# Key-product masks split between ScalarE and GpSimd, and the inverse's share per step changed

## The chip, the cores and the metric

The kernel runs on one core of a Trainium2 chip. The metric is device time in microseconds (us) from launch to end: the median of three runs of the kernel before is 1092.77 us (1090.2 to 1094.73). Engines: TensorE (PE; PEld its weight loads), VectorE (DVE), ScalarE (ACT), GpSimd (POOL) and SyncE (SP), which issues most DMAs.

## The reference

Three stages in float32: a linear recurrence per head (4 x 8 heads, 768 steps, head dimension 40), a mixture of experts, and a squared-ReLU feed-forward layer. Only the first is touched:

```python
for t in range(S):
    y[:, :, t] = einsum('bhd,bhde->bhe', rt, state)
    Sa = einsum('bhde,bhe->bhd', state, at)
    state_decay = state * wt[:, :, None, :] - einsum('bhd,bhe->bhde', Sa, bt)
    state = state_decay + einsum('bhd,bhe->bhde', vt, kt)
```

## The kernel before

The recurrence is cut into 24 chunks of 32 time steps, and four chunks make a slab. Within a chunk the recurrence is solved in closed form: the products of `k` and `b` with `a` give two 32 x 32 blocks a head, of which only the strictly lower triangles count (key products: rows 64 to 95 for `k`, rows 96 to 127 for `b`, the latter with the sign changed). The `b` block is inverted as a triangular matrix, one slab (four chunks of 32 heads, 128 partitions) at a time.

Names. `L(c)` makes the key products of chunk c: `heads` issues 32 matmuls of 40x64x32 (64 in the trace, fp32 counts twice) into the one PSUM tile `pr`, and then masks them into `zs` of that chunk; a DMA stores the `b` block in DRAM (`nt`), a later one (`tul`) reads it back turned into `tu`, on which `inv` works. `RUV` uses the same `heads` and the same `pr` for the products with `r` (R products), masked into `ym`; `Y` also writes to `pr`. So R, Y and the key products take turns in `pr`, and each must be evacuated before the next begins. `post` copies `a` into rows 0 to 39 of `zs` on ScalarE. `prod` scales `a` and `kb` of a chunk by decay products made by `decay` (four scans on VectorE for two chunks). In a chunk's own step `Zst`, `UTst`, `Ust`, `KBt`, `Sst`, `Stt` and `Y` do the matmul work, with ScalarE evacuating most of it and VectorE the state (`m`).

Every engine works in the order in which the program lists its instructions. That order is written out by hand: `ORD` lists, for a slab's first, second, third and fourth step (chunk index modulo 4), the stages of TensorE; behind each stage `pump` releases a number of places of a schedule, into which side work is put: `PA` says at which step, place and on which engines (V or G) `prod` of each chunk of the slab after next is issued, `LP` behind which stage its `L` stands. The first two `L` of a slab stand in the fourth step two slabs earlier, the other two in the first step of the slab before. `IB` gives the part of the inverse (in a planner's cost units) taken into each step: none in the first, the rest in the fourth. `IB0` does the same for the first slab's steps. The inverse for the next slab runs in a slab's second, third and fourth step.

In the profile below the steps are numbered by chunk: step 10 is a slab's third, step 11 its fourth, step 12 the first of the next slab.

Of the kernel before, what the change touches and what calls it, by code (L numbers as in the profile page):

```python
# [12 lines left out]
ALU = mybir.AluOpType  # L13
AF = mybir.ActivationFunctionType
# [3 lines left out]


class Attn:  # L20
    IB=(0, 6, 5, 99)
    IB0=(0, 7.5, 5.5, 99)
    I0=1
    PT=(2, 14)
# [2 lines left out]
    F2=5  # L27
    F3=0
    CA=(1, 2, 20)
    PA=((2, 11, 'VGG'), (2, 12, 'GGG'), (4, 4, 'VGG'), (4, 11, 'VGG'))  # L30
    CB=(3, 0, 20)
    SC=(2, 14)
    L0=('R', 'K0')
# [6 lines left out]
    def __init__(s, tc, ins, NC, ctx, ident, pctx=None, side=None):  # L40
        s.tc=tc; s.nc=nc=tc.nc; s.ins=ins; s.NC=NC; s.NS=NC//4
        P=lambda name,**k: ctx.enter_context(tc.tile_pool(name=name,**k))
        cp=s.cp=P('attn_c',bufs=1); cq=(pctx or ctx).enter_context(tc.tile_pool(name='attn_p',bufs=1,side=side))
        s.ps=P('aps',bufs=6,space=PSUM); s.psy=P('psy',bufs=1,space=PSUM)
        s.dram=P('adr',bufs=3,space=DRAM)
        T=lambda n,sh: cp.tile(sh,F32,tag=n,name=n)
        Tq=lambda n,sh: cq.tile(sh,F32,tag=n,name=n)
        def ring(n,k,sh,early=0): return [(Tq if i<early else T)(f'{n}{i}',sh) for i in range(k)]

        s.W=ring('w',2,[104,2,32,18],2); s.A=ring('a',4,[104,16,32],4); s.KB=ring('kb',8,[104,16,64],4)  # L50
        s.Pp=ring('pp',6,[104,2,32,18],4); s.Q=ring('qq',2,[104,2,32,18],2)
        s.one=Tq('one',[104,32,18]); s.inv_=Tq('inv',[104,32,18])
        s.ZS=ring('zs',8,[128,32,32],4)
        s.YS=T('ys',[128,32,40]); s.VU=T('vu',[128,32,40]); s.M1=T('m1',[128,32,64])
        s.YM=T('ym',[128,32,32]); s.R=T('r',[104,16,32]); s.UT=T('ut',[128,16,64]); s.UTc=T('utc',[128,2,256])
        s.TT=T('tt',[128,8,128]); s.TU=Tq('tu',[128,1024]); s.tmp=Tq('tmp',[128,256])
        s.Z=T('z',[128,8,64]); s.XT=T('xt',[104,4,16,32]); s.DL=ring('dl',12,[40,32])
        s.PR=s.psy.tile([128,2,512],F32,tag='pr',name='pr'); s.PY=[s.PR[:,i,256:512] for i in range(2)]
        s.ident=ident
        s.fill=[]; s.nt={}; s.td={}  # L60

        s.load_w(0); s.load_w(1); s.load_a(0); s.load_k(0); s.load_a(1); s.load_k(1)
        for c in (2,3): s.load_a(c); s.load_k(c)
        V=nc.vector; G=nc.gpsimd
        G.memset(s.one,0.0); G.memset(s.one[:,:,0:1],1.0); G.memset(s.one[:,:,17:18],1.0); G.memset(s.inv_,0.0)
        G.memset(s.TT,0.0)
        make_identity(nc,ident)
        s.mask=T('mask',[128,2,32])
        G.memset(s.mask,1.0); G.memset(s.mask[96:128,0],-1.0)
        for b in (64,96):  # L70
            G.affine_select(out=s.mask[b:b+32],in_=s.mask[b:b+32],pattern=[[0,2],[1,32]],compare_op=ALU.is_ge,fill=0.0,base=-1,channel_multiplier=-1)
        for t in s.ZS[0:2]: s.zero(t[32:64])
# [20 lines left out]
    r=0  # L93
# [36 lines left out]
    def post(s,c):  # L130
# [4 lines left out]
        if c:  # L135
            d=s.g(s.DL,c).rearrange('p (x r) -> p x r',r=2); pp=s.pslice(c-1)
            V.tensor_tensor(out=d[:,:,0],in0=pp[0:40,:,1,16],in1=q[0:40,:,0,0],op=ALU.mult)
            V.tensor_tensor(out=d[:,:,1],in0=pp[64:104,:,1,16],in1=q[64:104,:,0,0],op=ALU.mult)
    def heads(s,w,x,out,mask):

        nc=s.nc; pt=s.PR
        for p in range(8):
            for hf in range(2):
                for r in range(2):
                    k=slice(64*r,64*r+40)
                    nc.tensor.matmul(pt[64*hf:64*hf+64,r,32*p:32*p+32],w[k,8*hf+p,:],x[k,8*hf+p,:],start=True,stop=True)  # L146
        for hf in range(2):
            nc.vector.tensor_tensor(out=out[64:128,16*hf:16*hf+16].rearrange('p (x r) t -> p x r t',r=2),  # L148
                in0=pt[64*hf:64*hf+64,:,0:256].rearrange('p r (x t) -> p x r t',t=32),
                in1=mask.unsqueeze(1).unsqueeze(1).to_broadcast([64,8,2,32]),op=ALU.mult)  # L150
    def L(s,c,store=True):
        nc=s.nc; a=s.g(s.A,c); kb=s.g(s.KB,c); zs=s.g(s.ZS,c)
        s.heads(kb,a,zs,s.mask[64:128,0])
        sl=c//4
        if c%4==0: s.nt[sl]=s.dram.tile([4,32,32,32],F32,tag='nt',name='nt')
        if store: nc.sync.dma_start(s.nt[sl][c%4],zs[96:128])
        s.post(c); s.load_a(c+4)
# [105 lines left out]
    def run(s, sink, more=None, before=None):  # L263
# [27 lines left out]
        for c in range(NC):  # L291
# [18 lines left out]
            for P in (sl+1,sl+2):  # L310
# [4 lines left out]
                for k in range(4):  # L315
                    e,p,w=s.PA[k]
                    if d==e: at(p,lambda x=2*A+k,w=w: s.prod(x,eng(w)))
# [3 lines left out]
            if nx:  # L321
                ib=s.IB if sl else s.IB0
                if r==s.I0 if sl else r==1: s.invq=s.inv(sl+1)
# [530 lines left out]
```

## Time and profile before

| | us |
|---|---|
| median of three runs | 1092.77 |
| profiled execution | 1089.77 |
| its span | 1088.0 |
| PE, DVE, ACT, POOL busy | 911.3, 691.4, 463.8, 319.8 |

The span is the time from the first to the last instruction of one execution; the profiled execution's own time is 1.8 us longer. The chain of work that ended last is by 63% on PE, 16% on DVE, 5% on ACT and 2% on POOL. The recurrence takes the first 555 us or so; one slab of it repeats in steps 10 to 13, from 277.5 to 362.9. Busy time is an average over stages with different limits, so the steps are read one by one.

### The profile page before, as it was taken

How to read it: one execution, taken by the hardware profiler on the slowest of the kernel's cores; microseconds unless marked ns; L12 is line 12 of the kernel's file. 1: busy time of each engine (PE TensorE's matmuls, PEld its weight loads, DVE VectorE, ACT ScalarE, POOL GpSimd, SP SyncE). 2: the span in 40 equal slices, each digit the busy share in tenths (PEclk: the TensorE clock that was granted, in tenths of full speed). 3: DMA queues.
4: the chain of work that ended last, by engine and by line, in shares of the span. 5: the costliest groups of instructions: out<-in, count | busy, mean ns of one | idle time of the engine just before them, and what ended most of it. 6: DMA issues, size and time to landing. Idle time of an engine off the chain costs nothing.

```text
span 1088.0 us, 30273 instructions
## 1 busy us (share of the span) xinstructions
PE 911.3 (84%) x12696; PEld 867.5 (80%) x12696; DVE 691.4 (64%) x1621; ACT 463.8 (43%) x1016; POOL 319.8 (29%) x292
## 2 busy tenths in 40 slices
PE   1238978878978976998948989869999999999996
PEld 1227877777867866887848989869999999999996
DVE  7997967966875875864659988746444434443331
ACT  6324543543443443545536546424333333333331
POOL 6031512511521425536554223352121111100000
PEclk9999866866876876687859999989999999999999
DMA  7548674474464444459549887820011111000000
GB/s 183 129 105 237 185 186 119 114 189 114 117 165 113 110 115 126 107 152 261 146 141 256 285 300 254 251 83 20 25 30 31 30 31 31 28 29 13 13 12 17
DMA packets 128134, 132.05 MB, mean 121 GB/s; under 512 B 80201, under 2 KB 104559, under 8 KB 127987
## 3 DMA queue, kind: packets, MB, share of 16 engines
q1 hardware_dynamic: 123731, 118.95, 39.6%
q0 software_dynamic: 4256, 11.06, 3.1%
q8 instruction: 102, 1.67, 0.6%
q14 instruction: 45, 0.37, 0.1%
HBM read 104.79 MB, written 29.70 MB: 124 GB/s over the span
## 4 chain that ended last, share of the span: by engine, by line
PE 63%; DVE 16%; issue 6%; DMA 6%; ACT 5%; POOL 2%; SPq 1%; another core or an unknown queue 0%; ACTq 0%; DVEq 0%; POOLq 0%
PE fps L554 19%; PE fps L561 17%; PE ps L241 7%; PE pr L146 4%; PE ps L219 3%; PE pr L259 3%; PE ps L405 3%; PE ps L250 2%; PE ps L210 2%; DMA c<-in_w_out 2%; DVE tu L175 2%; DVE tmp L174 2%; POOL kb L129 1%; DVE ym L148 1%; DMA kb<-in_kb 1%
## 5 line engine op out<-in xcount | busy, mean ns | idle before, releaser
L554 PE MATMUL fps<-xl,w1h 128*128 128x256 f32 x768 | 198.8, 286 | 8.7 <-DVE xl L544 8.6
L554 PE MATMUL fps<-xh,w1h 128*128 128x256 f32 x768 | 199.8, 287 | 4.8 <-ACT xh L543 4.2
L561 PE MATMUL fps<-w2h,hh 128*128 128x320 f32 x512 | 158.7, 310 | 0.0
L561 PE MATMUL fps<-w2h,hl 128*128 128x320 f32 x512 | 158.2, 309 | 0.0
L561 PE MATMUL fps<-w2l,hh 128*128 128x320 f32 x512 | 158.1, 309 | 0.0
L554 PEld LDWEIGHTS fps<-xl,w1h 128*128 128x128 f32 x768 | 148.9, 194 | 10.5 <-DVE xl L544 10.5
L554 PEld LDWEIGHTS fps<-xh,w1h 128*128 128x128 f32 x768 | 148.7, 194 | 6.3 <-ACT xh L543 5.3
L662 DVE TENSOR_TENSOR g<-r 128x512 f32<-128x512 f32 x96 | 68.8, 716 | 81.0 <-ACT r L661 81.0
L664 DVE TENSOR_TENSOR hl<-g,hh 128x512 fp32r<-128x512 f32 x96 | 74.8, 779 | 66.0 <-ACT hh L663 65.3
L146 PE MATMUL pr<-a,kb 40*64 40x32 f32 x1536 | 43.2, 280 | 74.8 <-issue 29.8
L554 PE MATMUL fps<-xh,w1l 128*128 128x256 f32 x512 | 103.7, 284 | 0.0
L146 PEld LDWEIGHTS pr<-a,kb 40*64 40x64 f32 x1536 | 40.6, 206 | 78.4 <-issue 48.8
L663 ACT CAST hh<-g 128x512 fp32r<-128x512 f32 x96 | 59.6, 621 | 94.1 <-DVE g L662 94.1
L241 PEld LDWEIGHTS ps<-vu,ys 128*40 128x40 f32 x1472 | 89.0, 163 | 13.2 <-ACT ys L213 6.2
L241 PE MATMUL ps<-vu,ys 128*40 128x40 f32 x1472 | 94.3, 249 | 5.3 <-ACT ys L213 3.4
L561 PEld LDWEIGHTS fps<-w2l,hh 128*128 128x128 f32 x512 | 96.1, 188 | 0.0
L561 PEld LDWEIGHTS fps<-w2h,hh 128*128 128x128 f32 x512 | 96.1, 188 | 0.0
L561 PEld LDWEIGHTS fps<-w2h,hl 128*128 128x128 f32 x512 | 96.1, 188 | 0.0
L661 ACT ACTIVATE r<-fps 128x512 f32<-128x512 f32 x96 | 57.1, 595 | 76.6 <-PE fps L554 76.6
L554 PEld LDWEIGHTS fps<-xh,w1l 128*128 128x128 f32 x512 | 80.5, 194 | 0.0
L175 DVE TENSOR_TENSOR tu<-tu,tmp 128x120 f32<-128x120 f32 (+25 forms) x312 | 80.3, 292 | 0.0
L174 DVE TENSOR_TENSOR tmp<-tu 128x120 f32<-128x120 f32 (+25 forms) x312 | 74.5, 272 | 0.5
(143 smaller groups left out, 1739.8 us busy)
## 6 DMA issues: line engine op xcount, KB each, us to landing
kb<-in_kb SPq DMA_DIRECT2D x24, 416.0 KB
ut<-in_vE SPq DMA_DIRECT2D x24, 416.0 KB
raw<-in_w SPq DMA_DIRECT2D x16, 512.0 KB
raw<-in_w SPq DMA_DIRECT2D x16, 480.0 KB
w<-in_w SPq DMA_DIRECT2D x12, 468.0 KB
a<-in_a SPq DMA_DIRECT2D x24, 208.0 KB
r<-in_r SPq DMA_DIRECT2D x24, 208.0 KB
c<-in_w_out SPq DMA_DIRECT2D x7, 640.0 KB
```

The lines of the kernel that those rows point to most:

```text
L146: nc.tensor.matmul(pt[64*hf:64*hf+64,r,32*p:32*p+32],w[k,8*hf+p,:],x[k,8*hf+p,:],start=True,stop=True)
L174: if k==0: V.tensor_tensor(out=tv,in0=Tv[:,j:j+1,b0:b0+n].to_broadcast([128,j,n]),in1=Tv[:,0:j,j:j+1].to_broadcast([128,j,n]),op=ALU.mult)
L175: else: V.tensor_tensor(out=w,in0=w,in1=tv,op=ALU.add)
L219: nc.tensor.matmul(pt[32*i:32*i+32,40*j:40*j+40],zs[:,h,:],m[:,h,0:40],start=True,stop=True)
L241: nc.tensor.matmul(pt[k][0:40,40*n:40*n+40],ys[:,h,:],m[:,h,:],start=True,stop=True)
L259: nc.tensor.matmul(pt[64*par:64*par+40,32*(k//2):32*(k//2)+32],ys[:,h,:],ym[:,h,:],start=True,stop=True)
L554: nc.tensor.matmul(pt[:,256*u:256*u+256],a,b,start=i==0,stop=i==len(ops)-1)
L561: nc.tensor.matmul(pt[:,0:320],a,b,start=first and n==0,stop=last and n==23); n+=1
L661: nc.scalar.activation(out=r,in_=v,func=AF.Relu)
L662: V.tensor_tensor(out=g,in0=r,in1=r,op=ALU.mult)
L663: nc.scalar.copy(out=gh[:,2*m2:2*m2+2],in_=g)
L664: V.tensor_tensor(out=gl[:,2*m2:2*m2+2],in0=g,in1=gh[:,2*m2:2*m2+2],op=ALU.subtract)
```

## The change

Three edits. `heads` gets an argument `later`, true for the key products of chunks 4 to 23: instead of two VectorE multiplications by a mask of 0, 1 and -1, two ScalarE instructions copy the products from PSUM with a scale for each partition (`sgn`, 1 or -1), and two GpSimd instructions then set the part on and above the diagonal to zero in SBUF, 32 partitions each, the `b` block first. `IB` takes 8 instead of 5 units of the inverse in a slab's third step. `PA` gives the product of `a` of each slab's fourth chunk (from chunk 11 on) to GpSimd.

```diff
-    IB=(0, 6, 5, 99)
+    IB=(0, 6, 8, 99)
-    PA=((2, 11, 'VGG'), (2, 12, 'GGG'), (4, 4, 'VGG'), (4, 11, 'VGG'))
+    PA=((2, 11, 'VGG'), (2, 12, 'GGG'), (4, 4, 'VGG'), (4, 11, 'GGG'))
...
+        s.sgn=T('sgn',[128,1]); G.memset(s.sgn,1.0); G.memset(s.sgn[96:128],-1.0)
...
-    def heads(s,w,x,out,mask):
+    def heads(s,w,x,out,mask,later=False):
...
+        if later:
+            for hf in range(2):
+                nc.scalar.activation(out=out[64:128,16*hf:16*hf+16].rearrange('p (x r) t -> p x r t',r=2),
+                    in_=pt[64*hf:64*hf+64,:,0:256].rearrange('p r (x t) -> p x r t',t=32),func=AF.Copy,scale=s.sgn[64:128])
+            for b in (96,64):
+                nc.gpsimd.affine_select(out=out[b:b+32],in_=out[b:b+32],pattern=[[0,32],[1,32]],compare_op=ALU.is_ge,fill=0.0,base=-1,channel_multiplier=-1)
+            return
...
-        s.heads(kb,a,zs,s.mask[64:128,0])
+        s.heads(kb,a,zs,s.mask[64:128,0],c>3)
```

VectorE in the third step (step 10), around the mask of the R products (`ym`); `tu` and `tmp` are the inverse's, `a_87` the product of `a` for chunk 16, `m` the state's evacuation. Before:

```order
L174 TENSOR_TENSOR tmp<-tu 128x128
L174 TENSOR_TENSOR tmp<-tu 128x112
L175 TENSOR_TENSOR tu<-tu,tmp 128x16x8
L175 TENSOR_TENSOR tu<-tu,tmp 128x16x7
L148 TENSOR_TENSOR ym<-pr,mask 64x512 x2
L174 TENSOR_TENSOR tmp<-tu 128x119 x2
L175 TENSOR_TENSOR tu<-tu,tmp 128x17x7 x2
L408 TENSOR_REDUCE sm_198<-ps 128x9
L174 TENSOR_TENSOR tmp<-tu 128x126
L244 TENSOR_TENSOR m_119<-ps,dl_140 40x2x4x40 x2
```

And the same place of the changed kernel, whose lines stand some eight further down in the file:

```order
L182 TENSOR_TENSOR tmp<-tu 128x114 x2
L183 TENSOR_TENSOR tu<-tu,tmp 128x19x6 x2
L156 TENSOR_TENSOR ym<-pr,mask 64x512 x2
L182 TENSOR_TENSOR tmp<-tu 128x120
L182 TENSOR_TENSOR tmp<-tu 128x100
L183 TENSOR_TENSOR tu<-tu,tmp 128x20x6
L183 TENSOR_TENSOR tu<-tu,tmp 128x20x5
L182 TENSOR_TENSOR tmp<-tu 128x105
L416 TENSOR_REDUCE sm_201<-ps 128x9
L182 TENSOR_TENSOR tmp<-tu 128x105
L183 TENSOR_TENSOR tu<-tu,tmp 128x21x5
L252 TENSOR_TENSOR m_119<-ps,dl_140 40x2x4x40 x2
```

The inverse's columns 17 to 19 (four instructions each) moved from behind the R mask to ahead of it, and seven of its instructions stand between the mask and the first `m` where there were five.

GpSimd from the fourth step (step 11) into the first of the next slab (step 12); `xt` is the output's scaling, `kb` and `a` the products of later chunks, `xr`, `gt` and `xs` belong to the routing. Before:

```order
L262 TENSOR_TENSOR xt<-xt,pp_104 104x256 x2
L409 COPY xr_197<-xr_197 128x64
L129 TENSOR_TENSOR kb_93<-kb_93,qq_106 104x16x32 x2
L409 COPY xr_197<-xr_197 128x64
L129 TENSOR_TENSOR kb_94<-kb_94,qq_106 104x16x32 x2
L450 COPY gt_201<-xr_197 128x4
L428 DMA xs<-xr_197,slot 2048x388 x4
```

And after the change:

```order
L270 TENSOR_TENSOR xt<-xt,pp_104 104x256 x2
L153 AFFINE_SELECT zs_109<-zs_109 32x1024 x2
L153 AFFINE_SELECT zs_110<-zs_110 32x1024 x2
L417 COPY xr_200<-xr_200 128x64
L130 TENSOR_TENSOR kb_93<-kb_93,qq_106 104x16x32 x2
L417 COPY xr_200<-xr_200 128x64
L127 TENSOR_TENSOR a_90<-a_90,pp_102 104x512
L130 TENSOR_TENSOR kb_94<-kb_94,qq_106 104x16x32 x2
L153 AFFINE_SELECT zs_111<-zs_111 32x1024 x2
L153 AFFINE_SELECT zs_112<-zs_112 32x1024 x2
L458 COPY gt_204<-xr_200 128x4
L436 DMA xs<-xr_200,slot 2048x388 x4
```

Eight selects and one product of `a` came in, two selects behind each chunk's key products.

ScalarE in the first step (step 12), from the evacuation of U (`vu`) to the transposes of keys and state (`ys`), which the state products read. Before:

```order
L235 COPY vu<-ps 32x4x40 x8
L133 COPY zs_111<-a_89 40x16x32
L134 COPY zs_111<-a_89 40x16x32
L133 COPY zs_112<-a_90 40x16x32
L134 COPY zs_112<-a_90 40x16x32
L213 COPY ys<-ps 64x4x80 x2
L252 COPY ys<-ps 40x8x40 x2
```

And after the change:

```order
L243 COPY vu<-ps 32x4x40 x8
L150 ACTIVATE zs_111<-pr,sgn 64x512 x2
L134 COPY zs_111<-a_89 40x16x32
L135 COPY zs_111<-a_89 40x16x32
L150 ACTIVATE zs_112<-pr,sgn 64x512 x2
L134 COPY zs_112<-a_90 40x16x32
L135 COPY zs_112<-a_90 40x16x32
L221 COPY ys<-ps 64x4x80 x2
L260 COPY ys<-ps 40x8x40 x2
```

The copies of `a` moved behind the evacuation of each chunk's key products, and the transposes behind both.

## Rows read from the trace of the kernel before

**Rows 1.** Windows of steps 10, 11, 12: length, busy us (count) by engine, granted clock.

```profile
277.50:291.45 13.95, 12.66 (x314) 11.45 (x313) 10.88 (x34) 8.48 (x25) 9.78 (x8) 0.96 0.56 137
291.45:317.87 26.42, 19.62 (x475) 17.91 (x473) 21.49 (x68) 11.06 (x29) 8.38 (x5) 0.74 0.49 132
317.87:340.62 22.75, 18.58 (x416) 17.18 (x413) 13.09 (x37) 10.55 (x28) 2.75 (x4) 0.70 0.66 159
```

**Rows 2.** Timeline, TensorE, steps 11 and 12: start, length, work [idle before, releaser].

```profile
296.55 1.14 PE L146 MATMUL pr<-a,kb 40*64 40x32 f32 x64
302.54 1.90 PE L146 MATMUL pr<-r,ut 40*64 40x32 f32 x64 [2.84 <-DVE zs L148]
308.03 1.94 PE L146 MATMUL pr<-a,kb 40*64 40x32 f32 x64 [2.71 <-DVE ym L148]
327.57 1.94 PE L146 MATMUL pr<-a,kb 40*64 40x32 f32 x64 [2.00 <-DVE ym L148]
336.42 4.27 PE L241 MATMUL ps<-vu,ys 128*40 128x40 f32 x64
```

**Rows 3.** Timeline, VectorE, steps 10 to 12.

```profile
282.24 0.46 DVE L175 TENSOR_TENSOR tu<-tu,tmp 128x128 f32<-128x128 f32 x2
285.60 1.39 DVE L148 TENSOR_TENSOR ym<-pr,mask 64x512 f32<-64x512 f32 x2 [2.89 <-ACT vu L235]
287.02 1.69 DVE L174 TENSOR_TENSOR tmp<-tu 128x119 f32<-128x119 f32 x2
288.64 1.50 DVE L175 TENSOR_TENSOR tu<-tu,tmp 128x119 f32<-128x119 f32 x2
...
306.49 1.39 DVE L148 TENSOR_TENSOR ym<-pr,mask 64x512 f32<-64x512 f32 x2
...
323.43 1.19 DVE L437 TENSOR_TENSOR sm<-sm 128x32 f32<-128x32 f32 x1
326.03 1.39 DVE L148 TENSOR_TENSOR ym<-pr,mask 64x512 f32<-64x512 f32 x2
```

**Rows 4.** Timeline, GpSimd, steps 10 to 12.

```profile
280.22 3.69 POOL L262 TENSOR_TENSOR xt<-xt,pp 104x256 f32<-104x256 f32 x2 [4.17 <-ACT xt L261]
283.87 2.35 POOL L129 TENSOR_TENSOR kb<-kb,qq 104x512 f32<-104x512 f32 x2
287.34 2.43 POOL L129 TENSOR_TENSOR kb<-kb,qq 104x512 f32<-104x512 f32 x2
...
295.04 4.71 POOL L262 TENSOR_TENSOR xt<-xt,pp 104x256 f32<-104x256 f32 x1 [0.20 <-ACT xt L261]
...
322.20 2.38 POOL L129 TENSOR_TENSOR kb<-kb,qq 104x512 f32<-104x512 f32 x2
```

**Rows 5.** Timeline, ScalarE, step 12.

```profile
333.96 0.86 ACT L213 COPY ys<-ps 64x320 f32<-64x320 f32 x2 [4.08 <-PE ps L210]
335.70 0.87 ACT L252 COPY ys<-ps 40x320 f32<-40x320 f32 x2 [0.87 <-PE ps L250]
```

**Rows 6.** Groups by line and form, whole run: busy us, mean ns | idle before.

```profile
L148 DVE TENSOR_TENSOR zs<-pr,mask 64x512 f32<-64x512 f32 x48 | 33.1, 690 | 25.6 <-PE pr L146 25.1
L661 ACT ACTIVATE r<-fps 128x512 f32<-128x512 f32 x96 | 57.1, 595 | 76.6 <-PE fps L554 76.6
L133 ACT COPY zs<-a 40x512 f32<-40x512 f32 x24 | 14.8, 618 | 12.4 <-DVE a L126 8.6 <-issue 3.0 <-ACT zs L134 0.4
L727 POOL TENSOR_SCALAR c64m<-c64m 128x640 f32<-128x640 f32 x7 | 13.0, 1862 | 0.0
L66 POOL MEMSET tt<- 128x1024 f32 x1 | 1.0, 953 | 0.0
L71 POOL TENSOR_SCALAR_AFFINE_SELECT mask<-mask 32x64 f32<-32x64 f32 x2 | 0.5, 242 | 0.1
```

**Rows 7.** Timeline, VectorE, step 0.

```profile
72.33 1.39 DVE L148 TENSOR_TENSOR zs<-pr,mask 64x512 f32<-64x512 f32 x2 [1.69 <-PE pr L146]
```

**Rows 8.** Timeline, GpSimd, step 0.

```profile
79.94 5.47 POOL L129 TENSOR_TENSOR kb<-kb,qq 104x512 f32<-104x512 f32 x4 [17.50 <-DVE qq L113]
```

## The prediction

> **What bounds the kernel now.** I read the busy time by step first, then the timelines of TensorE, VectorE, GpSimd and ScalarE over one slab, then the durations by form. Only the attention part is touched. One slab of it (four chunks, four steps) repeats about every 85 us from the second on. I take steps 10, 11 and 12, a slab's third and fourth step and the first of the next [rows 1]. The third is bound by TensorE: 13.95 us, 12.66 of them busy, granted clock 0.96. The fourth is bound by VectorE: TensorE has 19.6 us of work in 26.4, much of it at 0.74 of the clock, and VectorE is busy for 21.5. The reader sees why in TensorE's timeline [rows 2]: the R products wait 2.84 us until VectorE has masked the key products of the slab after next (they share one PSUM tile), and the next key products wait 2.71 us for VectorE's mask of R. In the first step of the next slab there is one such wait, 2.00 us.
>
> VectorE's timeline says what it does meanwhile [rows 3]. It has a real pause only in the third step, 2.89 us ahead of the R mask at 285.60; from there to the R mask at 306.49 it goes from one instruction to the next, inverse, scans and masks in one queue. GpSimd's timeline [rows 4] holds the second thing to see: the two engines hold each other up. Two inverse instructions alone take 0.46 us at 282.24; at 287.02 two take 1.69 and the next two 1.50, just while GpSimd multiplies keys at 287.34. The other way round, GpSimd's 295.04 row lasts 4.71 us beside an unbroken row of inverse instructions. The R mask at 285.60 takes its usual 1.39 although GpSimd multiplies at that time (283.87 for 2.35, then on to 289.7): with PSUM as one input it is not held up.
>
> **The change, part by part.** From chunk 4 on, each chunk's key products lose two VectorE masks of 0.69 us [rows 6], 1.39 a chunk, and get two ScalarE instructions of 64x512 and two GpSimd selects of 32x1024. Twenty chunks: 27.8 us off VectorE's queue. What that is worth is read step by step.
>
> ScalarE's price has near rows [rows 6]: PSUM to SBUF with 512 columns 0.60, the copies of `a` into the same tile 0.62. I take 0.6, so 1.2 a chunk. A select of this size is not in the trace. Lower end: the same instruction on 64 columns, 0.24. Upper end: a GpSimd tensor_scalar of 640 columns at 1.86, scaled to 1024 2.98. I take 0.95, the memset of just 1024 columns on the same engine; 1.9 a chunk.
>
> *Fourth step (steps 3, 7, 11, 15).* Ahead of the R mask VectorE is rid of 1.39. But GpSimd's selects read SBUF, as its products do, and come while VectorE works through inverse and scans, which read two SBUF operands; by rows 3 each then holds up one VectorE instruction for about its own length. 1.9 - 1.39 = +0.5 us a step. Ends: -1.39 if the selects slip into gaps, 2 x 2.98 - 1.39 = +4.6 by the dear price. The page "SBUF — State Buffer" of the Trainium skill (Who interferes with whom) states this against the change: a VectorE instruction with two SBUF inputs and a GpSimd one that reads SBUF exclude each other for a whole instruction, one with at most one SBUF input is free of it. By that rule the old mask cost GpSimd nothing and the new select costs VectorE its full length; without it the term would be -1.39. The trace agrees for the products (1.69 against 0.46); no run here shows it for a select. The two ScalarE instructions also stand ahead of the second half of the inverse's U part and put it off by 1.2; that I cost at nothing, as R then comes at most 1.2 after the time TensorE could have had it, and it waited 2.84. If that cover goes, VectorE has already arrived (first rival), and the 1.2 is in its price.
>
> *Third step (steps 6, 10, 14, 18).* 46 instead of 28 inverse instructions stand here, 22 instead of 40 in the fourth. Twelve move ahead of the R mask, 12 x 0.2 = 2.4 us by row 282.24, into the 2.89 pause. The pause is not free, though: GpSimd uses it (283.87, two products). Its first row here, 280.22, took 3.69 for two, waiting for VectorE's row of instructions to end; with a longer row it starts about 2.4 later, at 285.0, and its seven instructions (2 x 0.6 by their 256 columns, 2.35 + 1.2 + 2.43: 7.2 us) then meet VectorE after the R mask, not in the pause. Before, 1.69 + 1.50 - 2 x 0.46 = 2.3 us were lost so. Now 5.2 of GpSimd's 7.2 lie behind the mask, which ends at 287.0, and VectorE gets five instructions of 0.2 through in that time: 4.2 lost. 4.2 - 2.3 - 2.4 = -0.5: next to nothing gained at the fourth step's end. But seven inverse instructions stand ahead of the first state evacuation instead of five: it comes at 287.0 + 5.2 + 0.6 = 292.8 instead of about 290.5 (row 288.64's end and 0.4), and TensorE's first product of the fourth step waits for it. The fourth step's own waits (2.84 and 2.71) mostly cover these 2.3. I take +0.4; ends -2.4 (all fits the pause) and +2.3 (not covered).
>
> *First step (steps 4, 8, 12, 16).* One product of `a`, 0.68 on VectorE, goes to GpSimd. There two products run now from 322.20 for 2.38, and the routing instruction at 323.43 takes 1.19 instead of 0.2; with a third, one more is held up by 1.2, so the R mask at 326.03 comes 1.2 - 0.68 = +0.5 later; I take +0.4, since R itself ends only just before. Then ScalarE [rows 5]: before, all four copies of `a` were done while it was idle (4.08 us ahead of 333.96). Now its queue is in order: products at 327.57 + 1.94 = 329.5, signs to 330.7, the fourth chunk's products to 332.9, signs to 334.1, copies 1.24 to 335.35, then the two key transposes 0.86 and the state transposes 0.87 to 337.1, which the state products wait for. They started at 336.42: +0.8 with the way to TensorE. Sum +1.2; ends 0 (copies slip, port free) and +2.2 (selects at the dear price holding up routing). Selects, the copy of the gates and the scatters share GpSimd's queue; the scatters wait for VectorE's slots far later, so they cost nothing. SyncE's store of each product waits for the select, and behind it stand the load of `a`, the read that turns the product, and loads for the next step; the inverse reads the turned product a step later, so 2 us there are covered.
>
> *First chunks (step 0).* VectorE's second mask waits 1.69 for TensorE [rows 7], and the scans behind it, for which GpSimd's products at 79.94 wait [rows 8], could start 1.39 + 1.69 + 1.39 = 4.5 earlier. Four selects (3.8) run beside the scans, and ScalarE's copies hold the state products back as above. I take -1.0, of -4.5 to +1.2.
>
> The sum: -1.0 + 4 x 0.5 + 4 x 0.4 + 4 x 1.2 = +7.4. The profiled execution took 1089.77 (span 1088.0 and 1.8 around it): 1097.2. The median, 1092.77, is 3.0 above it, so 1100 stands for the median of the changed kernel.
>
> **The rivals.** *Relief: the selects find gaps and the longer row fills the pause.* It decides at the R mask of the fourth step: from 306.49 by 1.39 and 2.4 to 302.7, and R itself, put off by ScalarE, ends at 302.54 - 2.84 + 1.2 + 1.9 = 302.8; with the mask and the way to TensorE its next products start at 304.4 instead of 308.03, -3.6 in three slabs, -1.4 in step 3. With the first chunks' -4.5 + 0.8 and ScalarE's +0.8 four times: -10.8 - 1.4 - 3.7 + 3.2 = -12.7, 1080. For it: VectorE is the bound there, and it loses work. Against: rows 287.02 and 323.43, where a neighbour on GpSimd costs VectorE more than a mask.
>
> *The longer row shuts GpSimd out and TensorE falls to its lower clock in the third step.* The state evacuation's 2.3 us come where TensorE is at 0.96 now. The same 64 products take 1.14 us at 296.55 (the 2.4 GHz level) and 1.94 at 308.03 (1.2 GHz), behind waits of two to three us. Some 7 us of products between 291.5 and 298.5 would take 4.8 more; TensorE would come to R at about 307 and to the next products 2.6 later. 4 x 2.6 + 4 x 1.2 = +15, 1108. Against: the fourth step has 5.5 us of waits to pay from.
>
> *Nothing reaches the end.* The selects cost what the masks cost, and TensorE's own work, slow in steps 11 and 12 alike, takes up the rest: 1093. For it: the masks' time is moved, not removed. Against: the engines it is moved to have other neighbours, so an even balance would be chance.
>
> **Chances.** Forecast 0.44 (its own range 1094 to 1106), relief 0.31, lower clock 0.12, nothing 0.13. Half a per cent, 5.5 us, is about what a measurement can tell from no change. Slower than 1098.2: three quarters of the forecast, 0.33, and most of the lower clock, 0.10: 0.43. Faster than 1087.3: nine tenths of relief, 0.28, and 0.01 of the last. The rest, 0.28, is within it. Range 1080 to 1112: from relief's whole price to the forecast with dearer selects in some steps.
>
> **What would show it.** Right: inverse instructions of over 1 us beside select rows; the select near 0.95; the first state product of a slab's first step waiting for ScalarE's `ys`; the first evacuation of the third step late behind inverse instructions. The steps of rows 1 should come to about 14.5, 26.5 and 24 us. Wrong: a fourth step under 24 us with the R products no longer waiting for VectorE, or selects of 0.3 us that VectorE does not feel; then relief holds. A granted clock well under 0.9 in the third step speaks for the second rival.

## The result, and the profile after

| | median us | range (runs) | profiled execution | span |
|---|---|---|---|---|
| before | 1093.16 | 1090.2 to 1095.89 (6) | 1089.77 | 1088.0 |
| changed | 1099.61 | 1096.97 to 1101.01 (6) | 1099.82 | 1098.1 |

The ratio is 1.0057, 95% interval 1.0036 to 1.0078: slower by 6 us. The forecast was 1100: +7.4 on the profiled execution, where +10.05 came, and 3.0 from there to the median. The medians differ by 6.45. Between the two traces all of the difference has arisen when the recurrence ends (10.3 us); the rest of the kernel takes as long as before.

The same three steps as in [rows 1], windows of the changed kernel (length, busy us of PE, PEld, DVE, ACT, POOL, granted clock, DMA share, GB/s):

```profile
286.92:302.85 15.93, 15.45 (x314) 14.28 (x312) 14.80 (x47) 8.47 (x25) 11.72 (x8) 0.72 0.51 124
302.85:328.16 25.31, 19.52 (x472) 17.88 (x472) 18.85 (x51) 13.89 (x33) 10.80 (x9) 0.73 0.52 136
328.16:351.46 23.30, 18.41 (x416) 16.79 (x413) 10.07 (x32) 13.29 (x32) 9.02 (x9) 0.71 0.64 154
```

The third step is 2.0 us longer, the fourth 1.1 shorter, the first 0.55 longer. TensorE's timeline of the changed kernel shows where it waits now (start, length, work, in brackets the idle time before and what ended it; the first row is the end of the third step one slab earlier, step 6):

```profile
215.02 1.04 PE L227 MATMUL ps<-m,zs 128*32 128x40 f32 x32 [1.83 <-DVE m L252]
...
297.80 4.77 PE L249 MATMUL ps<-vu,ys 128*40 128x40 f32 x64
302.85 1.04 PE L227 MATMUL ps<-m,zs 128*32 128x40 f32 x32 [0.29 <-DVE m L252]
...
312.26 0.44 PE L241 MATMUL ps<-ident,utc 40*128 40x40 f32 x6 [2.33 <-ACT utc L234]
312.63 1.73 PE L147 MATMUL pr<-r,ut 40*64 40x32 f32 x64
318.23 1.93 PE L147 MATMUL pr<-a,kb 40*64 40x32 f32 x64 [2.98 <-DVE ym L156]
337.93 1.93 PE L147 MATMUL pr<-a,kb 40*64 40x32 f32 x64 [2.06 <-DVE ym L156]
347.41 4.11 PE L249 MATMUL ps<-vu,ys 128*40 128x40 f32 x64 [0.58 <-ACT ys L260]
```

Against [rows 2]: the R products of the fourth step wait no longer for VectorE's mask (2.84) but for ScalarE, whose sign copies and copies of `a` stand ahead of U (2.33). The wait behind the R mask is about as long as before, 2.98 (2.71). New are the last wait, for the transposes that ScalarE evacuates after its sign copies, and the 0.29 at the start of the fourth step, for the evacuation of the state. That last one is short because TensorE is itself slow in step 10, at a granted clock of 0.72 with 15.45 us of work (12.66 before). In step 6 the clock is 0.97, and there the same wait is 1.83.

VectorE in the changed kernel, against [rows 3]:

```profile
296.78 2.46 DVE L182 TENSOR_TENSOR tmp<-tu 128x120 f32<-128x120 f32 x2
299.16 2.45 DVE L183 TENSOR_TENSOR tu<-tu,tmp 128x120 f32<-128x120 f32 x2
...
302.32 0.88 DVE L252 TENSOR_TENSOR m<-ps,dl 40x320 f32<-40x320 f32 x2
...
310.67 1.34 DVE L183 TENSOR_TENSOR tu<-tu,tmp 128x78 f32<-128x78 f32 x2
311.94 1.41 DVE L182 TENSOR_TENSOR tmp<-tu 128x54 f32<-128x54 f32 x2
...
316.69 1.39 DVE L156 TENSOR_TENSOR ym<-pr,mask 64x512 f32<-64x512 f32 x2
```

GpSimd in the changed kernel, against [rows 4], and its group of all selects (busy us, mean ns):

```profile
289.98 5.63 POOL L270 TENSOR_TENSOR xt<-xt,pp 104x256 f32<-104x256 f32 x2 [4.52 <-ACT xt L269]
295.57 2.35 POOL L130 TENSOR_TENSOR kb<-kb,qq 104x512 f32<-104x512 f32 x2
...
310.66 2.63 POOL L153 TENSOR_SCALAR_AFFINE_SELECT zs<-zs 32x1024 f32<-32x1024 f32 x2 [2.37 <-issue]
321.67 2.59 POOL L153 TENSOR_SCALAR_AFFINE_SELECT zs<-zs 32x1024 f32<-32x1024 f32 x2 [8.38 <-ACT zs L150]
```

```profile
L153 POOL TENSOR_SCALAR_AFFINE_SELECT zs<-zs 32x1024 f32<-32x1024 f32 x40 | 53.7, 1342 | 81.0 <-ACT zs L150 67.2 <-issue 12.4
```

Two pictures of one thing: the two engines hold each other up. In the third step GpSimd's first two instructions need 5.63 us (3.69 before), since VectorE's row of inverse instructions has grown; its products then run beside VectorE's next rows, pairs of which take 2.46 and 2.45 (1.69 and 1.50 in this place before, 0.46 undisturbed). In the fourth step two pairs at 310.67 and 311.94 take 1.34 and 1.41, just while the selects run; without selects such pairs take 0.36 and 0.27. A select takes 1.3 us.

ScalarE at the end of the first step, against [rows 5]:

```profile
343.38 1.38 ACT L150 ACTIVATE zs<-pr,sgn 64x512 f32<-64x512 f32 x2 [0.82 <-PE pr L147]
344.78 0.62 ACT L134 COPY zs<-a 40x512 f32<-40x512 f32 x1
...
346.94 0.86 ACT L260 COPY ys<-ps 40x320 f32<-40x320 f32 x2
```

It has no pause left between the last sign copy and the transposes.

### The profile page after: what moved, and what is told of

The parts are those of the page before. It is cut to its first block, busy times and chain, and to the rows that moved or that the text cites. A ratio compares the mean times of both kernels' runs of the same rounds, so it can differ in the third digit from the quotient of the medians.

```text
span 1098.1 us, 30339 instructions
## 1 busy us (share of the span) xinstructions
PE 914.3 (83%) x12696; PEld 870.1 (79%) x12696; DVE 685.6 (62%) x1577; ACT 491.5 (45%) x1056; POOL 382.9 (35%) x338
## 4 chain that ended last, share of the span: by engine, by line
PE 58%; DVE 20%; issue 7%; ACT 6%; DMA 6%; POOL 1%; SPq 1%; another core or an unknown queue 0%; ACTq 0%; POOLq 0%; DVEq 0%
PE fps L562 18%; PE fps L569 17%; PE ps L249 6%; PE pr L147 4%; DVE tu L183 4%; DVE tmp L182 3%; PE ps L227 3%; PE pr L267 3%; PE ps L413 2%; PE ps L258 2%; DMA c<-in_w_out 2%; DVE qq L114 1%; PE ps L218 1%; DVE ym L156 1%; ACT ys L260 1%
## 5 line engine op out<-in xcount | busy, mean ns | idle before, releaser
L562 PEld LDWEIGHTS fps<-xl,w1h 128*128 128x128 f32 x768 | 148.1, 193 | 15.2 <-DVE xl L552 15.2
L249 PEld LDWEIGHTS ps<-vu,ys 128*40 128x40 f32 x1472 | 91.5, 167 | 15.6 <-ACT ys L260 10.0
L249 PE MATMUL ps<-vu,ys 128*40 128x40 f32 x1472 | 96.8, 253 | 7.3 <-ACT ys L260 5.0
L183 DVE TENSOR_TENSOR tu<-tu,tmp 128x120 f32<-128x120 f32 (+25 forms) x312 | 88.7, 318 | 0.1
L182 DVE TENSOR_TENSOR tmp<-tu 128x120 f32<-128x120 f32 (+25 forms) x312 | 82.0, 296 | 0.4
L153 POOL TENSOR_SCALAR_AFFINE_SELECT zs<-zs 32x1024 f32<-32x1024 f32 x40 | 53.7, 1342 | 81.0 <-ACT zs L150 67.2
```

What stands on the lines that cost most here:

```text
L153: nc.gpsimd.affine_select(out=out[b:b+32],in_=out[b:b+32],pattern=[[0,32],[1,32]],compare_op=ALU.is_ge,fill=0.0,base=-1,channel_multiplier=-1)
L182: if k==0: V.tensor_tensor(out=tv,in0=Tv[:,j:j+1,b0:b0+n].to_broadcast([128,j,n]),in1=Tv[:,0:j,j:j+1].to_broadcast([128,j,n]),op=ALU.mult)
L183: else: V.tensor_tensor(out=w,in0=w,in1=tv,op=ALU.add)
L249: nc.tensor.matmul(pt[k][0:40,40*n:40*n+40],ys[:,h,:],m[:,h,:],start=True,stop=True)
L562: nc.tensor.matmul(pt[:,256*u:256*u+256],a,b,start=i==0,stop=i==len(ops)-1)
```

## The experiments

Twelve kernels, each timed in five rounds beside the kernel before on the same chip. The first eight of the table ran on chips on which the kernel before takes 1072 to 1074 us (the first kind below), the last four, like the runs above, on chips where it takes 1093 (the second kind; more in the last section); ratios are always to runs of the kernel before on the same chip. The only trace of the kernel before is from a chip of the second kind, so step lengths of the first eight kernels are not compared with [rows 1] without saying so.

| kernel | ratio to before | 95% interval |
|---|---|---|
| masks only | 1.0085 | 1.0055 to 1.0115 |
| inverse only | 1.0003 | 0.9981 to 1.0025 |
| `a` product only | 1.0020 | 0.9997 to 1.0043 |
| inverse and `a` product | 1.0018 | 0.9997 to 1.0038 |
| masks, no select | 0.9990 | 0.9966 to 1.0013 |
| masks, copies first | 1.0016 | 0.9991 to 1.0042 |
| masks in the fourth step only | 1.0038 | 1.0016 to 1.0061 |
| masks in the first step only | 1.0030 | 1.0003 to 1.0057 |
| changed, again | 1.0070 | 1.0044 to 1.0097 |
| masks, selects later | 1.0019 | 0.9991 to 1.0047 |
| masks, selects later, copies first | 0.9923 | 0.9891 to 0.9954 |
| changed, both repairs | 0.9990 | 0.9967 to 1.0012 |

### Which of the three edits

The masks alone: `IB` and `PA` as before.

```diff
-    IB=(0, 6, 8, 99)
+    IB=(0, 6, 5, 99)
-    PA=((2, 11, 'VGG'), (2, 12, 'GGG'), (4, 4, 'VGG'), (4, 11, 'GGG'))
+    PA=((2, 11, 'VGG'), (2, 12, 'GGG'), (4, 4, 'VGG'), (4, 11, 'VGG'))
```

> The new masks alone; the inverse's shares and the fourth a product as before. My theory (two selects cost VectorE about what two masks did, and ScalarE's copies of a, now behind the sign copies, hold up the state products of a slab's first step): first step about +0.7 us and fourth step between -1 and +0.5 in four slabs each, first chunks about 0: together 0 to +5, so 1093 to 1098. Rival, relief lost to the other two edits: the masks alone free VectorE by 1.4 us a chunk, the fourth step gets over 2 us shorter, time 1085 or less. Second rival, the masks are the whole loss: 1099.

The inverse alone, in the kernel before:

```diff
-    IB=(0, 6, 5, 99)
+    IB=(0, 6, 8, 99)
```

> Only the inverse's share in the third step changed (5 to 8). My theory: the third step gets longer by 1 to 2 us (GpSimd's products wait behind the longer inverse row and come later, after the R mask), the fourth shorter by about 1: in four slabs 0 to +4, so 1093 to 1097. Rival, the inverse's move pays: the fourth step is bound by VectorE and loses 18 instructions of 0.2 us, 3.6 us, the third has a pause for 12 of them: 1085 or less. Second rival, the move is the whole loss (TensorE's clock falls in the third step): 1098 or more.

The product alone, likewise with only the last entry of `PA` changed to `GGG`:

> Only the product of a of each slab's fourth chunk moved from VectorE to GpSimd. My theory: the R mask of the first step comes about 0.4 us later in four slabs, as GpSimd's third product holds up one more routing instruction by its length: +1 to +2, 1094 to 1095. Rival: nothing reaches the end, 1093. Rival: VectorE's 0.68 us is worth its length, 4 x -0.68, 1090.

And these two together:

> Both of these edits without the new masks. If the three edits add up, this is the kernel before plus the two differences measured alone. My theory: 1093 to 1099, and the masks' part is the changed kernel minus this one, 0 to +5. Rival (the edits need each other): the inverse's move only fits because the masks leave VectorE; then this one is slower than the changed kernel, over 1100.

On these chips the masks are the loss: 1.0085, 9 us, twice what the terms of the prediction for them give (-1.0 + 4 x 0.5 + 4 x 0.8 = 4.2); the second rival held, and the theory's 0 to +5 did not. The other two edits change nothing that can be told from no change, alone or together (1.0018, about the sum of 1.0003 and 1.0020, so without the masks they do not need each other). The three together were not run on these chips. Where each acts is seen when the key instants are taken relative to the first product of their step (worked out from the timelines, in slabs two to four; R mask in steps 7, 11, 15, first state product in 4, 8, 12, first state evacuation in 6, 10, 14; the first two rows are from chips of the second kind, the others of the first):

| kernel | R mask, fourth step | state products, first step | state evacuation, third step |
|---|---|---|---|
| before | 14.8, 15.0, 15.3 | 18.56, 18.56, 18.55 | 13.3, 13.0, 13.0 |
| changed | 13.8, 13.8, 13.9 | 19.25, 19.26, 19.25 | 15.2, 15.4, 15.6 |
| masks only | 15.2, 15.7, 15.9 | 19.19, 19.19, 19.18 | 13.1, 13.0, 13.0 |
| masks, no select | 14.1, 13.8, 14.1 | 19.17, 19.19, 19.19 | 13.0, 13.0, 13.0 |
| masks, copies first | 16.1, 15.7, 16.0 | 18.54, 18.53, 19.04 | 14.0, 14.0, 14.0 |
| inverse only | 13.3, 13.3, 13.3 | 18.55, 18.55, 18.57 | 16.3, 15.4, 16.4 |
| `a` product only | 14.6, 14.6, 14.7 | 19.01, 18.61, 18.61 | 13.1, 13.1, 13.0 |

The new masks make the R mask of the fourth step later although VectorE is rid of 1.39 us ahead of it, and the state products 0.64 later. The inverse's share makes the R mask 1.5 to 2.0 earlier and the state evacuation 2.4 to 3.4 later, and its time says that the two about cancel. Its windows of steps 10 and 11 are 41.14 us in sum. In [rows 1] it is 40.37, on the other kind of chip; the product-only kernel, on the same chip, has 41.88 there, so the windows decide nothing finer:

```profile
271.40:287.34 15.94, 15.60 (x315) 14.24 (x313) 14.59 (x48) 8.46 (x25) 11.49 (x8) 0.71 0.55 133
287.34:312.54 25.20, 19.82 (x473) 18.11 (x473) 19.69 (x55) 11.04 (x29) 5.55 (x5) 0.72 0.52 137
```

### Selects or ScalarE's order

Theory A, the selects hold VectorE up by the port; theory B, ScalarE's queue holds up TensorE. Without the selects:

```diff
-            for b in (96,64):
-                nc.gpsimd.affine_select(out=out[b:b+32],in_=out[b:b+32], ...)
```

> The masks-only kernel without the GpSimd selects: the triangles on and above the diagonal are not set to zero, so this leaves out part of the computation and prices it. Theory A (the selects hold up VectorE by the shared port; in the fourth step of the masks-only trace the R mask came 15.7 us after the step's start instead of 14.6 to 15.0): without them the R mask comes at 13 to 13.5 and the fourth step is over 1 us shorter in four slabs: 0.996 to 1.002 of the kernel before. Theory B (ScalarE's queue is the loss, through the copies of a behind the sign copies): no more than 0.002 below the masks-only kernel, so 1.006 or more.

With the copies of `a` ahead of the chunk's key products, for chunks 4 to 23:

```diff
+        if c>3: s.post(c)
         s.heads(kb,a,zs,s.mask[64:128,0],c>3)
...
-        s.post(c); s.load_a(c+4)
+        if c<=3: s.post(c)
+        s.load_a(c+4)
```

> The masks-only kernel with the copies of a of chunks 4 to 23 issued before the chunk's key products instead of behind their sign copies. Theory B: the state products of each slab's first step start 0.6 to 1.2 us earlier, the second half of U in the fourth step 1.2 earlier: 4 to 8 us in all, 1.001 to 1.005. Theory A alone: the first step gains its 0.7, the fourth nothing, as R's mask waits in VectorE's queue: -3 us, 1.005 to 1.006. If neither: 1.0085 as before.

Both theories hold, at different places, and neither is the whole loss: 0.9990 without the selects is below theory B's 1.006, and 1.0016 with the copies first is below the 1.005 of theory A alone. The same two pairs of inverse instructions and the R mask on VectorE, first in the masks-only kernel (step from 291.93), with the selects on GpSimd below them:

```profile
299.92 1.46 DVE L183 TENSOR_TENSOR tu<-tu,tmp 128x92 f32<-128x92 f32 x2
...
301.57 1.18 DVE L182 TENSOR_TENSOR tmp<-tu 128x96 f32<-128x96 f32 x2
...
307.66 1.39 DVE L156 TENSOR_TENSOR ym<-pr,mask 64x512 f32<-64x512 f32 x2
```

```profile
294.19 5.53 POOL L270 TENSOR_TENSOR xt<-xt,pp 104x256 f32<-104x256 f32 x2 [3.56 <-ACT xt L269]
299.79 2.71 POOL L153 TENSOR_SCALAR_AFFINE_SELECT zs<-zs 32x1024 f32<-32x1024 f32 x2
```

then without the selects (step from 286.40):

```profile
294.31 0.41 DVE L181 TENSOR_TENSOR tu<-tu,tmp 128x92 f32<-128x92 f32 x2
...
294.90 0.32 DVE L180 TENSOR_TENSOR tmp<-tu 128x96 f32<-128x96 f32 x2
...
300.15 1.39 DVE L154 TENSOR_TENSOR ym<-pr,mask 64x512 f32<-64x512 f32 x2
```

1.46 - 0.41 + 1.18 - 0.32 = 1.9 us lost to two selects, and the R mask comes 13.75 us after the step's start instead of 15.73. That is the mask's 1.39 saved and more than that paid. Theory A had the R mask at 13 to 13.5 without the selects; it came at 13.8 to 14.1, and the fourth steps (7, 11, 15) are 0.8 to 1.4 us shorter than with them. The page "SBUF — State Buffer" of the Trainium skill (Who interferes with whom) states such an exclusion for two-input SBUF instructions of VectorE; the trace agrees, and adds that VectorE lost 1.9 for 2.7 us of selects, not all of it.

In the first step the state products, masks only (step from 318.70) and copies first (step from 314.47):

```profile
337.89 4.80 PE L249 MATMUL ps<-vu,ys 128*40 128x40 f32 x64 [0.58 <-ACT ys L260]
```

```profile
333.51 4.53 PE L251 MATMUL ps<-vu,ys 128*40 128x40 f32 x64
```

The wait for ScalarE is gone, 19.19 has become 19.04 here and 18.53 in the step four chunks earlier: the old place. In the fourth step the edit did not do what was expected. The second half of U comes no earlier, since the copies of `a` stand ahead of it still, now before the sign copies instead of behind them. TensorE's wait there, masks only and then copies first:

```profile
301.33 0.45 PE L241 MATMUL ps<-ident,utc 40*128 40x40 f32 x6 [2.33 <-ACT utc L234]
```

```profile
295.90 0.45 PE L243 MATMUL ps<-ident,utc 40*128 40x40 f32 x6 [2.25 <-ACT utc L236]
```

In the first chunks (step 0) either edit takes 2.0 us off (47.4 to 45.4). Of the 9.3 us between the executions of masks only and copies first, step 0 and the first steps (4, 8, 12, 16) hold 5.2. The rest goes with TensorE's clock: the second steps are 4.3 shorter (granted clock 0.69 to 0.78 in step 9), the fourth 3.8 longer (0.74 to 0.69 in step 11), step 19 is 3.7 shorter (0.71 to 1.00). So theory B's wait is shown; its whole price is not.

Each edit alone brings the kernel to where the one before stands (0.999, 1.0016). The gains, 0.0095 and 0.0069, are together more than the loss of 0.0085: either they overlap, as in step 0, where either one gives the same 2.0, or the freed mask is worth something once both prices are gone. The two edits together were not run.

Then by place, the masks from chunk 8 on only for chunks whose key products stand in a fourth step (`c>7 and c%4<2` instead of `c>3`), or in a first step (`c>7 and c%4>1`):

> The new masks only for the first two chunks of each slab from chunk 8 on (those whose key products stand in a fourth step). Theory A: +0.4 to +1 us in each of four slabs, 1.002 to 1.004. Theory B: the fourth step has slack on ScalarE, so 1.000. A relief would be 0.998 or less.

> The new masks only for the last two chunks of each slab from chunk 8 on (key products in a first step). Both theories have ScalarE's order here, +0.7 to +1.2 us in each of four slabs: 1.003 to 1.005. If it is 1.000, the first step is not where the loss is, and what is missing lies in the first chunks (4 to 7).

1.0038 is as theory A had it and against theory B's 1.000; 1.0030 is at the lower end of what both had. 0.0085 - 0.0068 = 0.0017 is left for the first chunks, less than the intervals can tell.

### Repairs

The changed kernel again, for the sum of the edits:

> The changed kernel itself, beside the kernel before on the chip of this call, since the masks alone measured 1.0085. If the three edits add up, 1.0085 and 0.000 to 0.002 for the other two: 1.008 to 1.011. If the inverse's shorter part in the fourth step pays back some of what the selects cost there (R mask 13.8 us after the step's start in the changed kernel, 15.7 with the masks alone): 1.004 to 1.007.

1.0070, the lower of the two answers: together the edits cost no more than the masks alone, as far as ratios from the two kinds of chip can be compared. The shorter inverse row does pay in the fourth step, as the table's 13.8 against 15.2 to 15.9 shows.

Then the selects and the store of each slab's first chunk issued with the second's:

```diff
-        if store: nc.sync.dma_start(s.nt[sl][c%4],zs[96:128])
+        if c<4: ready=(c,)
+        else: ready={0:(),1:(c-1,c)}.get(c%4,(c,))
+        for x in ready:
+            if x>3: s.select(x)
+            if store: nc.sync.dma_start(s.nt[sl][x%4],s.g(s.ZS,x)[96:128])
```

> The masks-only kernel with the selects (and the store) of each slab's first chunk issued with those of its second, behind the R mask of the fourth step, where VectorE has some 4.5 us of pause. Nothing is left out. Theory A (the two selects cost where they stand beside the inverse and the scans): the R mask comes at 13.8 us after the step's start as without any select, not at 15.7: 0.999 to 1.003. If selects cost wherever they stand, or GpSimd's copy of the routing and its products behind them become late: 1.006 or more.

Here the edit missed its aim, and the trace says why. GpSimd has nothing else queued between the two chunks' selects, so an instruction that stands later in the program still runs when its data comes, right behind the sign copies at 305.11 to 306.48:

```profile
306.60 2.87 POOL L160 TENSOR_SCALAR_AFFINE_SELECT zs<-zs 32x1024 f32<-32x1024 f32 x2 [0.62 <-ACT zs L150]
```

The R mask comes 15.7 us after the step's start, as with the masks alone: the 13.8 that theory A expected did not come. Only the store has moved. That the time is in the range of theory A (1.0019) therefore says nothing for it. Against the trace of the kernel before, from a chip of the same kind, the masks' cost stands where the theories have it: the fourth steps (7, 11, 15) are 1.0 to 1.5 us longer and the first steps (4, 8, 12) 1.25 to 1.5, and the second steps, together 7.0 shorter, hide it. Whether the later store or the other chip makes the difference to 1.0085 stays open.

> Both repairs together: the selects of the first chunk behind the R mask, the copies of a ahead of the sign copies. Theory A and B add: 1.0085 - 0.007 - 0.006 = 0.995 to 0.998, faster than the kernel before by some 2 to 5 us: what VectorE's relief is worth once it is not paid for. Rival (one and the same loss was removed twice, the fourth step then waits for ScalarE's U part or the clock takes the gain): 0.999 to 1.002.

0.9923, faster than before by 7 to 8 us. But the fourth step's R mask stands at 14.9 to 15.2 and the state products at 18.54, as before. The time is gained elsewhere, in the second step, of which the windows are, before and then here:

```profile
255.40:277.50 22.10, 19.76 (x314) 17.19 (x313) 16.39 (x62) 7.95 (x23) 4.20 (x5) 0.64 0.41 110
```

```profile
256.82:275.02 18.20, 15.55 (x314) 13.75 (x312) 15.95 (x62) 7.93 (x23) 5.29 (x5) 0.81 0.50 132
```

3.9 us there and 4.0 in step 13, both at a granted clock of 0.81 instead of 0.64, with 15.55 us of TensorE's work instead of 19.76. So this is not the price of the relief, and a repeat on the other chips would be needed before calling it one.

> The changed kernel (all three edits) with both repairs: the first chunk's selects behind the R mask of the fourth step, the copies of a ahead of the sign copies. If the shorter inverse row of the fourth step and the freed VectorE add up, the R mask comes at 12 to 12.5 us after the step's start and the step is 1 to 1.5 us shorter than with the masks and repairs alone, against 1 to 2 us more in the third: 0.988 to 0.994. If the longer row of the third step costs what the fourth gains, as it did without the masks: 0.992 to 0.995. If TensorE's clock falls in the third step for good: 0.996 or more.

0.9990: from 1.0057 and 1.0070 back to the kernel before, as much as the copies of `a` gave in the masks-only kernel (0.0069). The R mask comes at 13.6, not at 12 to 12.5. By its time it is the third answer, but the reason given there fails: in steps 6 and 10 the granted clock is 0.79, and without the longer row it is 0.79 and 0.78.

What the longer row does is seen against the version without it, the one before (0.9923): the third steps 6, 10 and 14 are 1.2 to 1.4 us longer, step 18 4.3, the fourth steps 7, 11 and 15 1.2 to 1.5 shorter. So with the new masks, on these chips, the longer row and the `a` product cost 0.0067; without them, on the others, the two together cost 0.0018. Whether the masks or the chip makes that difference was not run.

How the row can cost so much is seen best at the last slab that has it. Step 18 of the changed kernel (changed, again), where GpSimd also prepares the expert weights; GpSimd, VectorE, TensorE:

```profile
465.89 7.14 POOL L270 TENSOR_TENSOR xt<-xt,pp 104x256 f32<-104x256 f32 x2
```

```profile
475.31 3.08 DVE L183 TENSOR_TENSOR tu<-tu,tmp 128x120 f32<-128x120 f32 x2
...
480.41 0.87 DVE L252 TENSOR_TENSOR m<-ps,dl 40x320 f32<-40x320 f32 x2
```

```profile
472.44 2.02 PE L413 MATMUL ps<-sel,xt 104*128 104x90 f32 x8 [2.14 <-POOL xt L270]
...
480.94 1.04 PE L227 MATMUL ps<-m,zs 128*32 128x40 f32 x32 [1.37 <-DVE m L252]
```

In the changed kernel's first trace the same two waits of TensorE, at a higher clock (0.82 instead of 0.73), are together 5.0 us:

```profile
469.36 2.02 PE L413 MATMUL ps<-sel,xt 104*128 104x90 f32 x8 [2.35 <-POOL xt L270]
...
477.87 1.04 PE L227 MATMUL ps<-m,zs 128*32 128x40 f32 x32 [2.66 <-DVE m L252]
```

GpSimd is shut out until VectorE's row ends, TensorE waits for it, then GpSimd's work meets VectorE's behind the R mask and the state evacuation is late: 19.3 us for this step in both traces, 14.06 before. With the inverse alone it took 14.98: there GpSimd's two products came through between VectorE's inverse instructions, in 0.80 and 0.82 us. So the step is not always hit; what decides that was not tried.

## Why the prediction was right, and which terms were not

The direction came out, and so did two of the mechanisms, the selects' and ScalarE's. That the time came out too (1100 for 1099.61) is in good part luck: the sum hides terms that err both ways. By place, from the starts of the steps in the two traces:

| steps | forecast, us | measured, us |
|---|---|---|
| first chunks (0) | -1.0 | +0.5 |
| first (4, 8, 12, 16) | +4.8 | +2.4 |
| third (6, 10, 14, 18), with what the row gives the fourth | +1.6 | +10.4 |
| fourth (3, 7, 11, 15) | +2.0 | -3.5 |
| second (5, 9, 13, 17) | not in the sum | +0.2 |
| 1, 2 and 19 to 22 | not in the sum | +0.4 |
| all | +7.4 | +10.3 |

Half of the measured sum is step 18 alone (+5.3, the 5.0 of waits above), where 0.4 was forecast. The three steps of [rows 1] were forecast at 14.5, 26.5 and 24 us and took 15.9, 25.3 and 23.3: 65.0 and 64.5 in sum, and no single one right.

By place, most of the loss on these chips stands where the longer inverse row works: third and fourth steps and step 19 give +5.6 of the 10.3. On the other chips the same edit alone cost nothing and the masks were the loss. Whether that is the chip, or the row and the masks beside each other, stays open; the three edits were not run there, nor the inverse alone here.

- *Selects in the fourth step: right, by the mechanism named.* 1.9 us for the pair, -1.39 for the masks, +0.5 forecast; the R mask of the masks-only kernel is 0.35 to 0.7 later than before in the same steps (0.6 to 1.2 later than in the product-only kernel, on the same chip). In the changed kernel the shorter inverse row covers it. The price of one was low (0.95, measured 1.3), but VectorE loses less than a select's length, and the two errors cancel, which is luck.
- *ScalarE's copies ahead of U in the fourth step: cost nothing, as forecast.* TensorE waits 2.33 for them where it waited 2.84 for the mask, and R starts 9.8 us after the step's start instead of 11.1.
- *ScalarE's queue in the first step: right.* +0.8 forecast, +0.69 measured (18.56 to 19.25), and the old instant again with the copies first.
- *Third GpSimd product in the first step: wrong.* +0.4 forecast for the R mask; it comes 8.22 us after the step's start instead of 8.16. One more routing instruction is held up, but by 0.66 (0.85 at 335.28, 0.20 before), not by 1.2, and that is what the 0.68 of the product paid for.
- *The longer inverse row: the late evacuation right, its cover wrong, the fourth step mis-sized.* The state evacuation is 2.4 us later in step 10 (12.98 to 15.40 after the step's start; 2.3 forecast; the row before is below, the one after is 302.32 above). That it then lengthens the third step is shown in step 6, where TensorE waits 1.83 for it; in step 10 the wait is 0.29, and the 2.0 us there are TensorE's own work at the lower clock as much as the evacuation. The forecast let the fourth step's waits cover nearly all of it; the third steps became longer by 1.0 to 5.3 instead. For the fourth step the text had "next to nothing gained at the fourth step's end"; the R mask is 1.5 to 2.0 earlier with this edit alone. Steps 10 and 11 together went from 40.37 to 41.24, +0.87, where +0.4 and +0.5 were forecast; steps 18 and 19 together by +3.9.

```profile
290.48 0.87 DVE L244 TENSOR_TENSOR m<-ps,dl 40x320 f32<-40x320 f32 x2
```

- *First chunks: no gain.* -1.0 forecast; step 0 took 47.48 instead of 46.97, and 45.4 with either cost taken away. Six kernels with the old masks there take 46.4 to 47.6, so the +0.5 is within what executions differ by, but a gain is not seen. The relief was there, and the costs ate it.
- *Second step: not in the sum.* Step 5 took 3.9 us more, step 17 3.5 less, with the granted clock (0.81 to 0.63, and 0.64 to 0.73); they happened to cancel.

On the chips where each edit ran alone, the masks' terms, 4.2 in sum, stand against 9 with an interval of 5.9 to 12.4: too small. The edits that were forecast to cost 1.6 (inverse) and 1.6 (product) cost 0.3 and 2 there, neither to be told from nothing. The rival of relief fell, but what spoke for it is true: without the selects the R mask is 0.7 to 1.3 us earlier than before, and yet, with ScalarE's cost still in it, the time is only that of the kernel before (0.999). That speaks for the rival's price of the freed mask having been too high.

The rival of the lower clock saw a real row: in step 10 the granted clock is 0.72 instead of 0.96, and the state products take 4.77 (3.4 before). But the longer row neither needs it nor makes it: in step 6 the changed kernel has the longer row at 0.97. The kernel with the `a` product alone shows the same in its step 10, the one with the masks alone does not:

```profile
275.21:291.04 15.83, 15.49 (x314) 14.20 (x313) 11.44 (x37) 8.45 (x25) 9.16 (x8) 0.72 0.57 135
```

```profile
278.13:291.93 13.80, 12.50 (x314) 11.29 (x313) 10.90 (x35) 8.48 (x25) 9.95 (x8) 0.97 0.60 147
```

and the former is the faster kernel. Where the clock is low moves from step to step between kernels.

## What to carry to other kernels

Work that is taken off a busy engine isn't free of it when the engine that takes it holds the first one up, as the selects did here (1.46 and 1.18 us for pairs that take 0.41 and 0.32): a VectorE instruction that reads PSUM can be the cheap one, and its replacement on GpSimd, from SBUF to SBUF, the dear one. Before moving an evacuation to another in-order engine, list what then stands behind it there; here four copies that had always been early became late, and putting them ahead took that wait away. A repair must be looked for in the trace, not in the time: an instruction that is only written later still runs when its data comes, if nothing is queued ahead of it. And a total that comes out says little of its terms: set them beside the trace step by step.

## What the runs showed of the hardware that was not expected

One program has two speeds by the chip it runs on: the kernel before takes 1072 to 1074 us on two chips and 1093 on others. The kernel before has no trace on a chip of the first kind, so where the difference lies can only be read from kernels near to it. The `a`-product kernel, one edit away, takes 67.4 us for its second steps (5, 9, 13, 17) on such a chip, the kernel before 85.4 on the other kind. The window that had 22.10 is there:

```profile
258.11:275.21 17.10, 15.22 (x314) 13.71 (x312) 16.26 (x62) 7.85 (x23) 5.65 (x5) 0.78 0.52 131
```

In the longer window TensorE waits six times for nothing that the profile shows (total us, times, longest):

```profile
PE pr L259 <- issue: 1.2, 3, 0.5
PE ps L250 <- issue: 0.7, 2, 0.5
PE ps L225 <- issue: 0.3, 1, 0.3
```

These waits are 2.2 us, and the shorter window has 1.8 of others, for ScalarE. So the waits themselves are not the difference: 4.5 of the 5.0 us are TensorE's busy time, 19.76 against 15.22, at a granted clock of 0.64 against 0.78. Behind the six waits its products run at the lower of its two levels, 1.2 GHz, as the R products show, in the longer window and then in the shorter one:

```profile
266.29 1.93 PE L146 MATMUL pr<-r,ut 40*64 40x32 f32 x64
```

```profile
264.54 1.14 PE L146 MATMUL pr<-r,ut 40*64 40x32 f32 x64
```

Why a chip has these waits, and why some kernels keep a higher clock on the same chip, the runs don't tell.
